# A slot plan for batches 3 to 8 of a fused window attention and SMELU network

## The chip, the cores and the metric

The kernel runs on one core of one Trainium2 chip. The metric is device microseconds (us) per execution, over the whole program: loads, attention, both matrix products, stores. Two sources of time are used: the median of three timed runs, and one profiled execution, from which every duration of a single instruction comes.

## The reference

```python
def _attn_ref(q, k, v):                       # 8 batches, 8 heads, 576 positions, head size 64
    scores = np.matmul(q, k.transpose(0, 1, 3, 2)) / np.sqrt(64)
    pos = np.arange(576)
    mask = np.abs(pos[:, None] - pos[None, :]) <= 32
    scores = np.where(mask, scores, -1000000000.0)
    attn = np.exp(scores - np.max(scores, axis=-1, keepdims=True))
    attn = attn / (np.sum(attn, axis=-1, keepdims=True) + 1e-09)
    return np.matmul(attn, v)
...
def _moe_ref(x, w_in, w_out):                 # x: 4608 tokens of 512; w_in 512 x 2048; w_out 2048 x 512
    h = x @ w_in
    g = np.where(h >= 1, h, np.where(h <= -1, 0.0, (h + 1) ** 2 / 4.0))
    return g @ w_out
```

The attention of each head looks only at positions at most 32 away. Its output, heads side by side, is the token matrix x (576 tokens per batch), and the SMELU network follows. All inputs and the output are float32 in memory; the kernel multiplies in bf16 and sums in float32.

## The kernel before

**Engines and the work.** TensorE does every product. ScalarE (ACT) does exponentials, logarithms, copies out of PSUM and half of SMELU. VectorE (DVE) does masks, normalisation and the other half. GpSimd (POOL) issues loads; SyncE (SP) issues stores and DMA transposes.

**The slot.** The outer loop (line 505) runs over 160 slots. Slots 0 to 143 each project a piece of tokens with `w_in`: up to slot 55 and from slot 136 a slot takes 256 tokens and 256 of the 2048 hidden columns (eight 128x256 matmuls, line 499); slots 56 to 135, the wide ones, take 512 tokens and 128 hidden columns (four 128x512 matmuls, line 524). Each fills one PSUM tile `hp`; the pool `ps_h` has two of them, so the projection of slot a needs the tile of slot a-2 to be free. SMELU of a slot has two forms. In a **plain** slot ScalarE makes `rr` = relu(h/2 + 1/2) (line 543), VectorE makes `mx` = max(h, rr) (line 549) and `gT` = min(rr, 1) * mx (line 550): `hp` is free after `mx`. In a **ScalarE-heavier** slot, named by the set `two_on_act`, ScalarE also squares `rr` (line 546) and VectorE does one operation (line 547): `hp` is free only after that.

**The products with w_out.** A unit (lines 441 to 464) is one 128x512 matmul of `gT` with `w_out`; sixteen make one tile of 128 tokens in a PSUM tile of `ps_o` (two buffers), which ScalarE copies out (line 463) and SyncE stores. Units are numbered through all tiles, and each slot issues the next few: four in slots 24 to 39, three in slots 40 to 71, four from slot 72 (lines 559 to 563; `post` before slot 40). The first 64 units' worth of work is done as "pairs" up to slot 23.

**The attention.** Each batch after the first is cut into five steps (`steps`, line 399). A step has a `scores` part and a `sums` part. `scores` (line 215): TensorE products of q and k, ScalarE `exp` into `pt` (line 239; line 268 for the tail of the sequence), VectorE mask (line 205) and, but for the tail, an addition `both` (line 244). `sums` (line 273): TensorE products of `pt` with v and with ones, then ScalarE `Ln` and `Exp` of minus that (lines 310 and 311: one over the sum), and a VectorE multiplication into the token matrix `xT` (lines 316 and 319). That multiplication is put off: `flush` issues it at the beginning of the next slot, ahead of that slot's `mx`. The list `sl` (line 420) holds one slot per remaining step; at slot `sl[n]`, between the projection and the units, `run` (line 483) issues the sums of step n and the scores of step n+1, which I call a **session**. A projection reads `xT` of all its tokens, so a session must be far enough ahead of the slot that needs it. Scores take one two-bank PSUM tile (`ps_s`) and sums another (`ps_n`).

**Loads.** For batches 3 to 7 `loads` names the slots at which GpSimd issues q, k and v, and `xps` those at which SyncE issues the DMA transposes of q and k. Neither queue waits for a slot as such: an instruction waits only for its place in the queue, its buffer and its data. Batches are numbered from 0 in the code, so "batches 3 to 8" of the change are b = 2 to 7.

**What sets the order.** The schedule is written by hand (`manual_schedule`): each engine runs its instructions in the order in which the program issues them, and the numbers in `sl`, `two_on_act`, the units per slot, `loads` and `xps` are the plan.

Of the kernel before, what the change touches and what calls it, by code (L numbers as in the profile page):

```python
# [14 lines left out]
def kernel(  # L15
# [20 lines left out]
    B, H, S, D = q.shape  # L36
    NT, DM, DFF = out.shape[0], 512, 2048
# [3 lines left out]
    MAIN = 480  # L41
    TAIL = S - MAIN
# [7 lines left out]
    nat = ctx.enter_context(tc.tile_pool(name="nat", bufs=2))  # L50
# [6 lines left out]
    ps_s = ctx.enter_context(tc.tile_pool(name="ps_s", bufs=1, space=bass.MemoryType.PSUM))  # L57
    ps_n = ctx.enter_context(tc.tile_pool(name="ps_n", bufs=1, space=bass.MemoryType.PSUM))
# [6 lines left out]
    band = const.tile([128, 192], BF, name="band")  # L65
# [7 lines left out]
    qTs = [const.tile([128, PAD + NY * S], BF, name=f"qT{i}") for i in range(3)]  # L73

    ctx.enter_context(tc.manual_schedule())
    V, P, A = nc.vector, nc.gpsimd, nc.scalar


# [24 lines left out]
    def load_v(b, n):  # L103
        if b not in vn:
            vn[b] = nat.tile([128, 2 * NC, 2, D], BF, name="vn", tag="vn", bufs=3)
        h, a = divmod(n, 2)
        y = NY * h + 2 * a
        nc.gpsimd.dma_start(out=vn[b][64 * a:64 * a + 64, :, h], in_=v[b, y:y + 2].rearrange("y s d -> (y s) d")  # L108
                            .rearrange("(c r) d -> r c d", r=64))
# [15 lines left out]
    for h in range(2):  # L125
# [8 lines left out]
    load_v(0, 0)  # L134
    P.affine_select(out=step, in_=step, compare_op=ALU.is_ge, fill=-1.0, base=-65, channel_multiplier=-1,
                    pattern=[[1, 257]])
    for n in range(1, 4):
        load_v(0, n)
    V.memset(ones, 1.0)
    for t in qTs:  # L140
        V.memset(t[:, 0:PAD], 0.0)
# [1 line left out]
    V.tensor_sub(band, step[:, 65:], step[:, :192])  # L143
    V.tensor_scalar(bias, band, 1.0, 2.0 ** 100, op0=ALU.subtract, op1=ALU.mult)

    def put(todo):
        for fn, *x in todo:
            fn(*x)

    cuts = [0, 256, 512, 768, 1024, 1280, 1536, DFF]  # L150
    w = [(load_w_in, c0, c1, h) for c0, c1 in zip(cuts, cuts[1:]) for h in range(2)]
    w[3] += ((0, 52, 64),)
    put(w[:4] + [(load_half, 1, t, h) for t in range(2) for h in range(2)] + w[4:])
    put([(load_w_out, 0, k, k + 4) for k in (0, 4, 8)] + [(load_rows, 1, t) for t in range(2)] + [(load_w_out, 0, 12, 16)])
    put([(load_v, 1, n) for n in range(4)])
    P.tensor_copy(band[HD[1], 0:128], band[HD[1], 64:192])
    for m, n, x in ((mask4, 8, 128), (mask8, 4, TAIL)):
        P.tensor_copy(m.rearrange("p (n j) -> p n j", n=n),
                      band[:, :x].rearrange("p (n j) -> p n j", n=1).to_broadcast([128, n, x]))
    put([(load_w_out, 1, 8 * n, 8 * n + 8) for n in range(2)])  # L160
    put([(load_nat, 2, t) for t in range(2)] + [(load_v, 2, n) for n in range(4)])


    kT = {}

# [221 lines left out]

    NB = NT // TB
    NF = DFF // 256
    pairs = [(7, 0), (7, 1), (8, 2), (11, 4), (12, 5), (13, 3), (15, 6), (15, 8), (16, 7), (17, 9)]  # L390
    two_on_act = (1, 7, 10, 11, 12)
    ev = {}

    def at(a, *todo):


        ev.setdefault(a, []).extend(x for x in todo if x)
# [5 lines left out]
                yield (sums, b, y1, lo, hi), (scores, b, (y1, y1 + 1), (0, 2), (2 * k, 2 * k + 2))  # L403
        yield (sums, b, 0, MAIN, S), (scores8, b)

    at(1, (tposes, 0, (0, 1), (1, 1)))
    at(2, (scores, 0, (0, 1), (0, 2), (2, 4)), (scores8, 0, ps_o))
    at(3, (scores, 0, (1, 2), (0, 2), (2, 4), ps_n), (sums, 0, 0, TB, MAIN, ps_s))
    at(4, (sums, 0, 1, TB, MAIN))
    at(5, (sums, 0, 0, MAIN, S, ps_s))  # L410
    seq = [x for b in range(1, B) for x in steps(b, CUT)]
    at(12.5, seq[0][1])
    at(13, (*seq[1][1], ps_n))
    at(14, (*seq[0][0], ps_s), seq[1][0])
    at(16, seq[2][1])
    for n, a in enumerate((18, 20, 26.5, 28)):
        at(a, seq[2 + n][0])
    for n, a in enumerate((18, 20, 26.5, 28)):
        at(a, seq[3 + n][1])
    sl = [30, 32, 35, 39, 42, 45, 47, 50, 52, 57, 60, 63, 66, 68, 72, 76, 79, 82, 86]  # L420
    sl += [90, 93, 96, 100, 104, 108, 111, 114, 118, 123]
    for n, a in enumerate(sl):
        at(a, seq[6 + n][0], seq[7 + n][1] if n < len(sl) - 1 else None)
    for t in range(2):
        at(10 + 1.5 * t, (tposes, 1, (t, 0), (t, 1)))
    two_on_act += tuple(a + 2 for a in sl)
    loads, xps = {}, {16: [(2, 0)], 18: [(2, 1)]}
    for b in range(LONG + 1, B):
        a = sl[5 * (b - 1) - 7] - 17
        for t in range(3):  # L430
            loads.setdefault(a + t, []).append((b, t))
        for t in range(2):
            xps.setdefault(a + 6 + 2 * t, []).append((b, t))

    op = {}

# [4 lines left out]
    def unit(x):  # L441

        tt, j = divmod(x, 16)
        if tt == NT // 128 - 1:
            half, n = divmod(j, 8)
            if n == 0:
                op[tt] = ps_o.tile([128, 256], FP, name="op", tag="op")
            cols = slice(256 * half, 256 * half + 256)
            for k in (2 * n, 2 * n + 1):
                nc.tensor.matmul(op[tt], gT[:, k, home(tt // 2), 128 * (tt % 2):128 * (tt % 2) + 128], w_out[:, k, cols],  # L450
                                 start=k == 0, stop=k == 15)
            if n == 7:
                osb = osp.tile([128, 256], FP, name="osb")
                A.copy(osb, op[tt])
                nc.sync.dma_start(out=out[128 * tt:128 * tt + 128, cols], in_=osb)
            return
        if j == 0:
            op[tt] = ps_o.tile([128, DM], FP, name="op", tag="op")
        nc.tensor.matmul(op[tt], gT[:, j, home(tt // 2), 128 * (tt % 2):128 * (tt % 2) + 128], w_out[:, j],  # L459
                         start=j == 0, stop=j == 15)  # L460
        if j == 15:
            osb = osp.tile([128, DM], FP, name="osb")
            A.copy(osb, op[tt])  # L463
            nc.sync.dma_start(out=out[128 * tt:128 * tt + 128, :], in_=osb)
# [18 lines left out]
    def run(pos):  # L483
        todo = []
        for fn, *x in ev.get(pos, []):
            if fn is sums:
                todo.append(sums(*x))
            elif fn is tposes:
                tposes(*x)
            else:  # L490
                pool = (x.pop(),) if x[-1] in (ps_s, ps_n, ps_o) else ()
                fn(*x, eng, *pool)
        for end in todo:
            end()

# [5 lines left out]
                             skip_group_check=True)  # L501

    hps = []
    done = 4 * (40 - NF)
    for a in range(NF * NB + 2 * NF):
        wide = WIDE[0] <= a < WIDE[1]
        eng = None if a < 14 else V
        post = [] if a >= 40 else [x for n, x in pairs if n == a] + [a - NF] * (a >= 2 * NF + 2)
        for b, x in loads.get(a, []):
            if x < 2:  # L510
                load_nat(b, x)
# [38 lines left out]
                V.scalar_tensor_tensor(g, rr, 1.0, mx, op0=ALU.min, op1=ALU.mult)  # L550
        flush()
        run(a)
        for x in post:
            if x < 16:
                pair(x)
            else:
                for j in range(4):
                    unit(4 * x + j)
        if a >= 40:
            n = 3 if a < 72 else 4  # L560
            for x in range(done, done + n):
                unit(x)
            done += n
        run(a + 0.5)
        for x in xps.get(a, []):
            xpose(*x)
# [30 lines left out]
```

## Time and profile before

| What | Value |
|---|---|
| median of three runs | 307.9 us (307.62 to 308.05) |
| profiled execution, whole time | 307.01 us |
| span of its profile (first to last instruction) | 305.2 us |
| granted TensorE clock | 1.00 throughout |
| VectorE busy | 232.4 us, 144 SMELU slots among it: 110 plain, 34 ScalarE-heavier |
| ScalarE busy | 208.0 us |
| TensorE, first matmul to last start | 1.19 to 301.55 us |
| slot 29 starts (its projection) | 72.86 us |
| slot 56, the first wide one, starts | 124.24 us |
| slot 144 onwards: only units | from about 287 us |

The profile gives each instruction's busy time, the idle time before it, and what released it. A matmul's listed duration (0.38 us for 128x512) is its latency: matmuls are pipelined, and the distance from one start to the next (0.216 us for the same one) is what it costs the engine. So the share "PE 97%" does not tell whether TensorE loses time; the starts do.

### The profile page before, as it was taken

The numbers are of one execution on the slowest core, as the hardware profiler recorded it, in microseconds if no ns is written. First come the engines' busy times: TensorE is split into PE (matmuls) and PEld (weight loads), VectorE is DVE, ScalarE is ACT, GpSimd is POOL, SyncE is SP. The second block draws the span as 40 slices with busy tenths as digits, with TensorE's granted clock in tenths as the row PEclk, the third lists the DMA queues.
The fourth block names the chain that finished last, engine by engine and source line by source line (L and its number), as shares of the span: only waits on it lengthen the run. The fifth ranks groups of instructions, "written<-read, shape, count | busy, mean of one in ns | idle before, by whom it ended". The sixth has DMA issues, their size and how long they took to land.

```text
span 305.2 us, 7779 instructions
## 1 busy us (share of the span) xinstructions
PE 296.6 (97%) x3268; PEld 172.1 (56%) x3268; DVE 232.4 (76%) x377; ACT 208.0 (68%) x347; POOL 77.5 (25%) x93
## 2 busy tenths in 40 slices
PE   8889999999999999999999999999999999999995
PEld 3467878876566667545444444444445444446644
DVE  4269878989888898999888878877888877788700
ACT  3677786738877888788877877786778755444311
POOL 8895771019008107303700640000000000000000
PEclk9999999999999999999999999999999999999999
DMA  9999999999999999996999998570101000000121
GB/s 151 182 180 200 187 183 172 173 165 147 135 213 90 172 159 128 150 147 121 165 133 156 120 173 82 113 114 34 37 34 38 37 35 37 35 34 34 63 77 69
DMA packets 137251, 35.66 MB, mean 117 GB/s; under 512 B 122240, under 2 KB 132992, under 8 KB 137216
## 3 DMA queue, kind: packets, MB, share of 16 engines
q0 software_dynamic: 103056, 18.06, 80.5%
q1 hardware_dynamic: 34016, 16.81, 27.2%
q8 instruction: 25, 0.41, 0.6%
q10 hardware_dynamic: 144, 0.29, 0.4%
q14 instruction: 10, 0.08, 0.1%
HBM read 36.70 MB, written 9.44 MB: 151 GB/s over the span
## 4 chain that ended last, share of the span: by engine, by line
PE 84%; DMA 4%; DVE 4%; POOL 4%; ACT 2%; issue 1%; POOLq 0%; ACTq 0%
PE op L459 33%; PE hp L524 23%; PE hp L499 14%; PE op L474 5%; PE bb L304 5%; DMA w_in<-in_moe_w_in_dram 4%; POOL w_in L113 2%; PE bb L231 2%; DVE mx L549 1%; PE op L450 1%; POOL vn L108 1%; ACT pt L239 1%; DVE gT L550 1%; PE tp L191 1%; DVE xT L316 1%
## 5 line engine op out<-in xcount | busy, mean ns | idle before, releaser
L543 ACT ACTIVATE rr<-hp 128x512 f32<-128x512 f32 x144 | 85.5, 594 | 68.5 <-PE hp L524 37.7
L459 PE MATMUL op<-w_out,gT 128*128 128x512 bf16 x496 | 127.0, 380 | 0.0
L549 DVE TENSOR_TENSOR mx<-hp,rr 128x512 f32<-128x512 f32 x110 | 75.8, 689 | 26.1 <-ACT rr L543 25.3
L524 PE MATMUL hp<-xT,w_in 128*128 128x512 bf16 x320 | 82.1, 379 | 0.0
L550 DVE SCALAR_TENSOR_TENSOR gT<-rr,mx 128x512 bf16<-128x512 f32 x110 | 76.4, 694 | 3.8
L459 PEld LDWEIGHTS <-gT 128*128 128x128 bf16 x496 | 46.0, 98 | 47.6
L499 PE MATMUL hp<-xT,w_in 128*128 128x256 bf16 x512 | 66.4, 273 | 3.3 <-DMA w_in<-in_moe_w_in_dram 2.1
L499 PEld LDWEIGHTS <-w_in 128*128 128x128 bf16 x512 | 49.1, 98 | 19.0 <-issue 3.2
L524 PEld LDWEIGHTS <-w_in 128*128 128x128 bf16 x320 | 31.2, 98 | 38.2 <-issue 0.9
L100 POOL DMA_DIRECT2D qn<-in_q_dram x12 | 14.6, 1223 | 91.7 <-DMA kT<-kn 89.6
L239 ACT ACTIVATE pt<-bb 128x1024 bf16<-128x1024 f32 (+1 forms) x33 | 32.8, 999 | 3.5 <-PE bb L231 2.2
L547 DVE SCALAR_TENSOR_TENSOR gT<-hp,mx 128x512 bf16<-128x512 f32 x34 | 23.5, 690 | 13.9 <-ACT mx L546 13.6
L108 POOL DMA_DIRECT2D vn<-in_v_dram x32 | 27.5, 893 | 6.1 <-DMA w_out<-in_moe_w_out_dram 3.2
L463 ACT COPY osb<-op 128x512 f32<-128x512 f32 x31 | 18.0, 579 | 12.0 <-PE op L459 11.6
L316 DVE TENSOR_TENSOR xT<-bb,rc 128x512 bf16<-128x512 f32 (+1 forms) x32 | 20.9, 654 | 5.7 <-ACT rc L311 5.6
L311 ACT ACTIVATE rc<-lr 128x512 f32<-128x512 f32 (+2 forms) x40 | 23.5, 588 | 1.3
L310 ACT ACTIVATE lr<-bb 128x512 f32<-128x512 f32 (+2 forms) x40 | 22.0, 550 | 0.2 <-PE bb L304 0.2
L546 ACT ACTIVATE mx<-rr 128x512 f32<-128x512 f32 x34 | 21.4, 630 | 1.1
L205 DVE TENSOR_TENSOR pt<-pt,mask 128x1024 bf16<-128x1024 bf16 (+1 forms) x33 | 20.3, 615 | 1.4 <-ACT pt L239 1.4
L304 PE MATMUL bb<-pt,vn 64*64 64x128 bf16 (+3 forms) x712 | 18.7, 207 | 0.0
L304 PEld LDWEIGHTS <-vn 64*64 64x64 bf16 x712 | 14.7, 107 | 4.9 <-issue 4.7
L474 PE MATMUL op<-w_out,gT 128*128 128x256 bf16 x128 | 16.4, 273 | 0.0
(63 smaller groups left out, 167.2 us busy)
## 6 DMA issues: line engine op xcount, KB each, us to landing
out_dram<-osb SPq DMA_DIRECT2D x35, 256.0 KB, 2.8
vn<-in_v_dram POOLq DMA_DIRECT2D x32, 144.0 KB, 11.2
qn<-in_q_dram POOLq DMA_DIRECT2D x12, 288.0 KB, 6.2
kn<-in_k_dram POOLq DMA_DIRECT2D x12, 288.0 KB, 8.8
w_in<-in_moe_w_in_dram POOLq DMA_DIRECT2D x11, 128.0 KB, 5.1
w_out<-in_moe_w_out_dram POOLq DMA_DIRECT2D x4, 256.0 KB, 9.2
w_out<-in_moe_w_out_dram POOLq DMA_DIRECT2D x2, 512.0 KB, 12.3
kh<-in_k_dram POOLq DMA_DIRECT2D x4, 144.0 KB, 5.1
```

Source lines behind the costliest of these rows:

```text
L108: nc.gpsimd.dma_start(out=vn[b][64 * a:64 * a + 64, :, h], in_=v[b, y:y + 2].rearrange("y s d -> (y s) d") .rearrange("(c r) d -> r c d", ...
L239: A.activation(p, ps[:, :, :w * n].rearrange(like, y=m), AF.Exp, scale=D ** -0.5)
L304: nc.tensor.matmul(bb[HD[h], a, o + c0:o + c1], ones[HD[a]] if c is None else vn[b][HD[a], c, h], p(a, h), start=n == 0, stop=True, skip_g ...
L311: A.activation(rc[:, :, :D0], lr[:, :, :D0], AF.Exp, scale=-1.0)
L316: muls.append(lambda: V.tensor_mul(o, bb[:, :, :D0], rc[:, :, :D0]))
L459: nc.tensor.matmul(op[tt], gT[:, j, home(tt // 2), 128 * (tt % 2):128 * (tt % 2) + 128], w_out[:, j], start=j == 0, stop=j == 15)
L474: nc.tensor.matmul(o[:, tt], gT[:, j, p, 128 * tt:128 * tt + 128], w_out[:, j, 256 * half:256 * half + 256], start=not done, stop=len(done ...
L499: nc.tensor.matmul(hp[:, j], w_in[:, kk, 256 * f + 128 * j:256 * f + 128 * j + 128], xT[:, kk, r0:r0 + TB], start=first and n == 0, stop=l ...
L524: nc.tensor.matmul(hp.rearrange("p n t -> p (n t)"), w_in[:, kk, 128 * f:128 * f + 128], xT[:, kk, r0:r0 + 2 * TB], start=n == 0, stop=n == 3)
L543: A.activation(rr, hp, AF.Relu, scale=0.5, bias=0.5)
L549: V.tensor_max(mx, hp, rr)
L550: V.scalar_tensor_tensor(g, rr, 1.0, mx, op0=ALU.min, op1=ALU.mult)
```

## The change

The number of instructions on TensorE, GpSimd and SyncE stays the same. From slot 24 on the plan has other numbers, now in tables:

- **Sessions.** `sl` has as many entries, 29, at other slots: the second and third move from 32 and 35 to 35 and 37, for instance, and the last from 123 to 117. In the wide slots sessions lie between 58 and 117 instead of 57 and 123.
- **ScalarE-heavier slots.** `two_on_act` was "two slots after every session" and becomes a list: 24 slots in all instead of 34. From slot 29 on there are 19 instead of 29, six of them after the last session (122, 123, 126, 127, 131, 132).
- **Units.** `units` gives 0 to 7 per slot. The running total differs from that of before by at most four, and is the same at the end.
- **Order in a session.** At the slots of `ends_first` the logarithm and its `Exp` come ahead of the exponential of the new scores. Of its eight slots only 49 and 89 hold a session.
- **Loads and transposes.** They get other slots. The order on the queues of GpSimd and SyncE, instruction by instruction, is the same as before.
- The lists `LOADS`, `early_items` and `pairs` write out what was computed; up to slot 23 nothing changes but the slot of one batch's loads.

```diff
-    two_on_act = (1, 7, 10, 11, 12)
...
-    sl = [30, 32, 35, 39, 42, 45, 47, 50, 52, 57, 60, 63, 66, 68, 72, 76, 79, 82, 86]
-    sl += [90, 93, 96, 100, 104, 108, 111, 114, 118, 123]
+    two_on_act = [1, 7, 10, 11, 12, 30, 34, 41, 44, 47, 51, 59, 62, 64, 74, 90, 96, 109, 122, 123, 126, 127, 131, 132]
+    sl = [30, 35, 37, 39, 42, 45, 47, 49, 52, 58, 60, 63, 65, 68, 71, 77, 79, 81, 85, 89, 92, 95, 101, 103, 108, 110, 112, 115, 117]
+    first_sl = 6
+    bias_until = 14
+    ends_first = [36, 49, 75, 89, 93, 116, 118, 123]
     for n, a in enumerate(sl):
-        at(a, seq[6 + n][0], seq[7 + n][1] if n < len(sl) - 1 else None)
...
+        at(a, seq[first_sl + n][0], seq[first_sl + 1 + n][1] if first_sl + 1 + n < len(seq) else None)
-    two_on_act += tuple(a + 2 for a in sl)
...
-        a = sl[5 * (b - 1) - 7] - 17
+        a = [20, 31, 49, 72, 88][b - 3]
...
-            xps.setdefault(a + 6 + 2 * t, []).append((b, t))
+            xps.setdefault([[28, 30], [40, 44], [58, 59], [75, 79], [91, 98]][b - 3][t], []).append((b, t))
...
             if fn is sums:
                 todo.append(sums(*x))
+                if pos in ends_first:
+                    todo.pop()()
...
-    done = 4 * (40 - NF)
+    done = 64
+    units = [0, 0, 0, 0, 0, 0, 0, 0, 0, 0, 0, 0, 0, 0, 0, 0, 0, 0, 0, 0, 0, 0, 0, 0, 5, 3, 5, 4, 5, 3, 6, 5, 0, 4, 4, 5, 4, 4, 3, 3, 3, 4, 3, 3, 3, 3, 2, 4, 3, 1, 5, 3, 2, 3, 4, 3, 2, 3, 4, 2, 4, 3, 3, 3, 4, 3, 3, 2, 4, 3, 4, 1, 4, 6, 2, 5, 2, 4, 5, 3, 4, 4, 5, 4, 6, 2, 2, 7, 2, 4, 6, 4, 4, 2, 4, 3, 5, 4, 5, 4, 6, 1, 3, 6, 4, 5, 4, 3, 3, 5, 5, 2, 4, 7, 2, 4, 0, 4, 5, 6, 3, 6, 3, 7, 4, 2, 5, 4, 3, 4, 4, 4, 4, 4, 5, 4, 2, 4, 6, 3, 4, 3, 4, 4, 5, 2, 4, 4, 6, 5, 4, 5, 3, 2, 3, 3, 4, 7, 4, 4]
...
-        if a >= 40:
-            n = 3 if a < 72 else 4
-            for x in range(done, done + n):
-                unit(x)
-            done += n
+        for x in range(done, done + units[a]):
+            unit(x)
+        done += units[a]
```

## Prediction

> **What bounds the kernel now.** I read the page first. TensorE is busy 97% and carries 84% of the chain that ended last; VectorE and ScalarE are busy 76% and 68%.
>
> ```profile
> PE 296.6 (97%) x3268; PEld 172.1 (56%) x3268; DVE 232.4 (76%) x377; ACT 208.0 (68%) x347; POOL 77.5 (25%) x93
> ...
> PE 84%; DMA 4%; DVE 4%; POOL 4%; ACT 2%; issue 1%; POOLq 0%; ACTq 0%
> ```
>
> The busy share counts latency, so I went to the timeline of TensorE and looked at starts. Four w_out products take 0.864 us from first start to next work, eight narrow projection matmuls 0.87, four wide ones 0.864: 0.216 us per 512 columns, with nothing between. So TensorE streams, and the question is only where it does not. From slot 29 on I find seven places where a projection starts later than the work before it allows. The largest is slot 32, the second slot 50:
>
> ```profile
> 77.95 1.03 PE L459 MATMUL op<-w_out,gT 128*128 128x512 bf16 x4
> 78.82 0.38 PE L499 MATMUL hp<-xT,w_in 128*128 128x256 bf16 x2
> 79.76 0.81 PE L499 MATMUL hp<-xT,w_in 128*128 128x256 bf16 x6 [0.56 <-DVE xT L316]
> ```
>
> ```profile
> 110.98 0.81 PE L459 MATMUL op<-w_out,gT 128*128 128x512 bf16 x3
> 111.63 1.04 PE L499 MATMUL hp<-xT,w_in 128*128 128x256 bf16 x8
> 112.50 0.81 PE L459 MATMUL op<-w_out,gT 128*128 128x512 bf16 x3
> 113.55 1.03 PE L499 MATMUL hp<-xT,w_in 128*128 128x256 bf16 x8 [0.24 <-DVE mx L549]
> ```
>
> In slot 32 two matmuls start from 78.82, so the third was due at 79.04; it starts at 79.76 when VectorE has written `xT`: 0.72 us lost. In slot 50 three units from 112.50 take 0.65 us (110.98 to 111.63 shows it), so 113.15 was due and 113.55 came: 0.40. The same reading gives 0.17 at 122.72 (slot 55), 0.07 at 131.11 and 136.46 (60, 63), 0.09 at 141.87 (66) and 0.19 at 151.01 (71). All others lose at most 0.03. The sum, 1.71 us, is all that a new order of the same matmuls can win: number and shape of TensorE's 3268 matmuls stay, and what is lost before slot 29 (the w_in loads at 14.8, 18.4 and 26.1) is untouched.
>
> **What the change costs, engine by engine.** Ten slots become plain. Each gives VectorE one more operation (`mx`, 0.69 us) and takes a square (0.63) from ScalarE: VectorE +6.9 us busy, ScalarE -6.3. Whether that costs anything depends on how closely VectorE can run, which the burst after a session shows:
>
> ```profile
> 236.37 0.69 DVE L550 SCALAR_TENSOR_TENSOR gT<-rr,mx 128x512 bf16<-128x512 f32 x1
> 236.98 0.69 DVE L205 TENSOR_TENSOR pt<-pt,mask 128x1024 bf16<-128x1024 bf16 x1
> 237.70 0.42 DVE L244 TENSOR_TENSOR both<-pt 128x512 bf16<-128x512 bf16 x1
> 238.04 0.69 DVE L316 TENSOR_TENSOR xT<-bb,rc 128x512 bf16<-128x512 f32 x1
> 238.65 0.68 DVE L549 TENSOR_TENSOR mx<-hp,rr 128x512 f32<-128x512 f32 x1
> 239.36 0.69 DVE L550 SCALAR_TENSOR_TENSOR gT<-rr,mx 128x512 bf16<-128x512 f32 x1
> ```
>
> The reader is to see the starts: an operation that needs its predecessor follows after 0.72 us, an independent one already after 0.61 (0.34 after `both`), 0.08 before the listed end. So a plain slot costs VectorE 0.72 + 0.61 = 1.33 us, a ScalarE-heavier one 0.61, a session 0.72 + 0.34 + 0.60 = 1.66 (tail scores: 0.28 for mask and no `both`). TensorE's side: 0.87 per projection, 0.216 per unit, about 0.75 for a session (slot 73 before: 2.48 us from projection to projection, its neighbours 1.73).
>
> I summed both over stretches of the new plan. Slots 64 to 71: TensorE 8 x 0.87 + 24 x 0.216 + 2.2 for three sessions = 14.3 us; VectorE 7 x 1.33 + 0.61 + 2.3 (masks, `both`) + 1.7 (`xT`) = 13.9 (before: 13.5 and 11.4). Slots 81 to 89: 17.8 against 15.3. Slots 108 to 117, five sessions: 19.9 against 18.2. ScalarE stays below 15 in all of these. Nowhere does VectorE need more than TensorE gives; over the worst short stretch (66 to 72) it falls back 0.8 us. Between sessions the projection comes 1.07 us after its tile is free (`mx` of slot 126 ends 259.03, the projection of slot 128 starts 260.10), so 0.8 is covered. **Throughput: nothing; what it costs if that cover fails is the second rival.**
>
> **Latency around sessions** is what makes the small losses. From the last score matmul run, `exp`, `Ln`, `Exp`, `xT` and the next slot's `mx` follow each other: after the session of slot 42 scores end at 100.29, `mx` at 103.92, so 3.63. The projection three slots on comes after two projections and the units of three slots: 1.74 + 0.216 U. With U = 9 that is 3.68: 0.05 to spare. Before, all ten sessions of the three-unit zone have U = 9; a heavier slot at the wrong place, or a copy of a finished tile (0.57), tips them over. The new plan gives U: 13, 10, 10 (slots 35, 37, 39), 9, 9, 8, 9, 9 (42 to 52), 10, 10, 10, 8, 11, 11 (58 to 71), and 10 or more later, but for 8 at 115. The two eights at 65 and 115 are tail sessions, whose `exp` takes 0.49 instead of 1.02 us; the eight at 47 has the next session within its three slots.
>
> - Slot 32: the session of slot 30 stays, but 11 units instead of 8 lie between its scores and slot 32: +0.65 us, and one more unit has been done by slot 29 (0.22, which delays both). Square first: `rr` about 75.9 to 76.5, square to 77.1, `exp` from 77.05, `Ln`, `Exp` to 79.1, mask from 78.1 and `both`, `xT` 79.1 to 79.75. The third matmul of slot 32 is due at 79.9. 0.72 goes. What is late next: slot 33 follows with no unit between, at 80.55, and its tile is free at about 80.4; slot 34 has 0.2 to spare.
> - Slot 50: ScalarE runs without pause from 105.72 (session 45) to `rr` of slot 48 at 112.08. From that session to slot 50 TensorE now has 13 units instead of 15 but one session more: -0.43 + 0.65 = +0.22. 0.18 of the 0.40 stays.
> - Slot 52: from session 49 (tail; `Ln` first) I get `mx` of slot 50 at 117.1 against a projection due at 117.0: 0.1.
> - Slots 55, 60, 63, 66, 71: the square leaves slot 52 (now 51, so the session's `exp` starts 0.4 earlier), and U is 9 there but 10 to 11 at 58, 60, 63, 68: 0.216 more each, against 0.07 to 0.19. All go: 0.59.
> - Heavier slots hold their tile longer: `rr` + square + 0.69 + gaps = 2.18 against 0.87 + 0.216 (two slots' units). That needs 6.1 units or a session between; 4 to 5 plus session at 30 to 64, 7 at 74, 10 and 11 at 122 and 123 hold it. 96 has 0.1 to spare.
>
> Remaining: 0.28 worked out, and I add 0.2 for what such sums miss in slots with 0.1 to 0.2 to spare. Bounds: 0 (all the new spaces hold) to 1.7 (every one that has at most 0.2 to spare fails by as much as slot 71 did, 0.19, nine times). Sum: 1.71 - 0.48 = **1.2 us won**.
>
> **Moved loads and transposes**: nothing. All five batches' loads wait for the transpose before them, not for a place in the program (GpSimd waits 89.6 us for `kT<-kn`, five times), and both queues keep their order. Transposed k lands at 115.95 for batch 4, its scores start at 118.53; after the change about 0.85 earlier, 117.7, still 1.7 us behind. For batch 7 the k transpose now waits for a store one slot later (before: 200.70, landed 206.35); scores at about 212.3. The end (units, copy, store from 287) is the same.
>
> **A rule against it.** VectorE waits 25.3 us for `rr` at line 549 and 13.6 us for squares at line 547, so it has room for 6.9. The Trainium skill (Perfetto Trace Analysis, section Identifying the Most-Contended Engine) says that matmul occupancy does not measure TensorE's distance from its limit, and that occupancy does for VectorE. By that, VectorE with its 76% would be the engine to relieve, and this change loads it: the rule's sum would be up to +6.9 us. The starts 0.216 us apart speak for TensorE, and I go by them.
>
> **Rivals.**
> 1. The gain is eaten by new small waits. Twenty-five sessions with a tenth or two to spare each; for it speaks that U varies by slot and sessions now follow at two slots' distance; against it that spaces are wider than before nearly everywhere. If 1.1 to 1.7 remains instead of 0.48, it gives 307.3 to 307.9, say 307.5.
> 2. VectorE becomes the bound, slower. If independent operations in dense stretches followed after their listed time plus 0.035 us (plain slot 1.45, session 1.9 to 2.0), slots 36 to 72 would need 4.1 us more VectorE than TensorE time (before: 1.3 at most, slots 42 to 64, where 0.99 was lost). Lost there about 3.8, against 1.71 won: +2.1, 310.0. It decides from a pitch of about 0.67 on: each 0.01 more adds 0.1 to 0.15 over slots 66 to 72, whose 0.8 then passes the 1.07 and 0.3 of the sums' own error. Against it: every burst in the timeline has independent starts 0.61 apart.
> 3. It does not do what it says: "ScalarE-heavier" stands for ten such slots fewer. That is in the sums already and gives no time of its own.
>
> **Numbers.** The profiled execution took 307.01 (span 305.2 and 1.8 around it), 0.9 below the median 307.9; I apply the difference to the median: 307.9 - 1.2 = **306.7 us**, in a profile a span of about 304.0. Chances: forecast 0.66, rival 1 0.21, rival 2 0.13. 0.2% is 0.6 us, about what can be told from no change, so faster means below 307.3: 0.66; same 0.21; slower 0.13. Range: 305.9 (all 1.71 and 0.3 of scatter, as the three runs show) to 308.2 (rival 1 whole, and the scatter).
>
> **What would show it.** In the new timeline no wait for `xT` at slot 32 and at most a tenth or two at 50 and 52; projections and units back to back from slot 53 on; VectorE busy about 239, ScalarE 202; slot 144 starting some 1.2 us earlier. Wrong if the wait list shows TensorE behind line 549's successor by more than 1 us in all, above all at slots 64 to 72, 85 to 88 or 112 to 118, or behind `kT` at 52.

## The result and the profile after

The changed kernel took 305.52 us (median of 20 runs), the kernel before 307.94 beside it (20 runs). The ratio is 0.9945 with a 95% interval of 0.9926 to 0.9963: 1.7 us faster, between 1.1 and 2.3 (the two medians lie 2.4 apart and the two means 2.1, so the medians overstate it). Set against the 307.9 of the prediction, the ratio gives 306.2. Single runs spread from 304.7 to 307.5, more than the effect, so most of what follows is read from traces: there every lost tenth has a place. The profiled execution took 305.21 us, with a span of 303.4 (before 305.2).

The page of the changed kernel: busy times, the shares of the chain that ended last, and two groups of SMELU instructions on VectorE (count, then busy us and mean ns, then idle time before and its releaser). Line numbers are new: L446 is a unit, L488 and L512 the narrow and the wide projection, L295 the sums' products, L222 the scores' products, L307 the writing of `xT`, L537 and L538 the plain slot's `mx` and `gT`, L535 the one operation of a ScalarE-heavier slot.

```profile
PE 295.3 (97%) x3268; PEld 172.3 (57%) x3268; DVE 236.5 (78%) x387; ACT 200.6 (66%) x337; POOL 77.8 (26%) x93
...
PE 89%; DMA 4%; POOL 4%; DVE 1%; issue 1%; ACT 0%; POOLq 0%; ACTq 0%
...
L537 DVE TENSOR_TENSOR mx<-hp,rr 128x512 f32<-128x512 f32 x120 | 82.5, 688 | 22.6 <-ACT rr L531 21.3
...
L535 DVE SCALAR_TENSOR_TENSOR gT<-hp,mx 128x512 bf16<-128x512 f32 x24 | 16.6, 690 | 10.6 <-ACT mx L534 10.0
```

TensorE now carries 89% of the chain instead of 84%, and VectorE 1% instead of 4%: the hand-overs to VectorE that ended the idle time of TensorE have gone, although VectorE itself has become busier (236.5 us, 232.4 before).

TensorE's waits for VectorE from its first projection or score on, in the changed kernel (what it waited for: us in total, times, longest; waits for loads, all ahead of slot 29, are left out here):

```profile
PE hp L488 <- DVE xT L307: 0.5, 1, 0.5
PE bb L222 <- DVE kT L185: 0.2, 1, 0.2
PE bb L295 <- DVE xT L307: 0.2, 1, 0.2
```

The first two lie ahead of slot 29, at 13.4 and 8.5 us, in the part that the change does not touch. From slot 29 on one wait is left, in the sums of the session at slot 47. Slot 32, the largest loss before, shows how one went; TensorE's timeline (start, us, line, tiles, count):

```profile
77.39 1.04 PE L488 MATMUL hp<-xT,w_in 128*128 128x256 bf16 x8
78.26 1.24 PE L446 MATMUL op<-w_out,gT 128*128 128x512 bf16 x5
79.34 1.91 PE L488 MATMUL hp<-xT,w_in 128*128 128x256 bf16 x16
```

Five units take 5 x 0.216 = 1.08, and 78.26 + 1.08 = 79.34: slot 32 starts when it can, and its sixteen matmuls (slot 32 gives no units, so slot 33 joins it) run as one group. `xT` was written from 78.81 to 79.43, in time for the third of them. The wait that is left, in TensorE's timeline and in VectorE's:

```profile
106.08 0.59 PE L446 MATMUL op<-w_out,gT 128*128 128x512 bf16 x2
106.51 1.04 PE L488 MATMUL hp<-xT,w_in 128*128 128x256 bf16 x8
107.70 0.31 PE L295 MATMUL bb<-pt,vn 64*64 64x128 bf16 x8 [0.15 <-DVE xT L307]
```

```profile
104.63 0.69 DVE L537 TENSOR_TENSOR mx<-hp,rr 128x512 f32<-128x512 f32 x1 [0.17 <-ACT rr L531]
105.36 0.69 DVE L538 SCALAR_TENSOR_TENSOR gT<-rr,mx 128x512 bf16<-128x512 f32 x1
105.97 0.68 DVE L196 TENSOR_TENSOR pt<-pt,mask 128x1024 bf16<-128x1024 bf16 x1
106.68 0.42 DVE L235 TENSOR_TENSOR both<-pt 128x512 bf16<-128x512 bf16 x1
107.03 0.62 DVE L307 TENSOR_TENSOR xT<-bb,rc 128x448 bf16<-128x448 f32 x1
```

The sums of session 47 were due 0.96 after the projection (0.87, and 0.09 to the sums as elsewhere), at 107.47; they came at 107.70: 0.22 lost (the bracket says 0.15, since it counts from the modelled end of the matmuls). What they wait for is not `xT` as data. The sums have one PSUM tile (`ps_n`), and it is free only when session 45's `xT` has been read out of it, at 107.65. Slots 45 and 46 give 3 + 2 units where they gave 3 + 3, and one unit, 0.216, is the whole wait.

Where the time went, by starts on TensorE:

| Start of | before | after | difference |
|---|---|---|---|
| slot 24 | 62.60 | 62.26 | -0.34 |
| slot 29 | 72.86 | 72.95 | +0.09 (two more units are done by then: +0.43) |
| slot 40 | 95.63 | 94.35 | -1.28 |
| slot 56 | 124.24 | 122.83 | -1.41 |
| slot 104 | 214.43 | 213.38 | -1.05 |
| slot 143 | 286.07 | 284.06 | -2.01 |
| last matmul | 301.55 | 299.75 | -1.80 |
| slot 29 to last | 228.70 | 226.81 | -1.89 |

Between slots the running number of units differs by up to four, 0.86 us, so single rows swing; the last row is the clean one. Of its 1.89, 0.43 are the two units that moved ahead of slot 29. The rest, 1.46, is close to what the waits say: 1.71 before, 0.22 after. Of the 1.80 between the two profiled executions, 0.34 lie ahead of slot 24, where both kernels do the same work.

That gives a measure for every kernel below. Without waits the stretch from slot 29 to the last matmul would be 228.70 - 1.71 = 226.99 us with the even units of before, and 226.81 - 0.22 = 226.59 with the new ones. What a kernel's stretch has above that is **lost by the stretch**; what single starts show, as in the prediction, is **lost by starts**. Both come from the starts of one trace and the measure is set by the two complete traces, so they check each other place by place and are not independent proofs.

### The profile page after: what moved, and what is told of

Its sections match the earlier page's. It is cut to its first block, busy times and chain, and to the rows that moved or that the text cites. A ratio compares the mean times of both kernels' runs of the same rounds, so it can differ in the third digit from the quotient of the medians.

```text
span 303.4 us, 7774 instructions
## 1 busy us (share of the span) xinstructions
PE 295.3 (97%) x3268; PEld 172.3 (57%) x3268; DVE 236.5 (78%) x387; ACT 200.6 (66%) x337; POOL 77.8 (26%) x93
## 4 chain that ended last, share of the span: by engine, by line
PE 89%; DMA 4%; POOL 4%; DVE 1%; issue 1%; ACT 0%; POOLq 0%; ACTq 0%
PE op L446 36%; PE hp L512 23%; PE hp L488 16%; PE bb L295 5%; PE op L461 5%; DMA w_in<-in_moe_w_in_dram 4%; PE bb L222 2%; POOL w_in L114 2%; POOL vn L109 1%; PE op L437 1%; PE tp L182 1%; POOL kh L88 0%; DVE mx L537 0%; DVE gT L538 0%; PE bb L201 0%
## 5 line engine op out<-in xcount | busy, mean ns | idle before, releaser
L446 PE MATMUL op<-w_out,gT 128*128 128x512 bf16 x496 | 126.6, 380 | 0.0
L537 DVE TENSOR_TENSOR mx<-hp,rr 128x512 f32<-128x512 f32 x120 | 82.5, 688 | 22.6 <-ACT rr L531 21.3
L538 DVE SCALAR_TENSOR_TENSOR gT<-rr,mx 128x512 bf16<-128x512 f32 x120 | 83.3, 694 | 4.1
L512 PE MATMUL hp<-xT,w_in 128*128 128x512 bf16 x320 | 82.0, 379 | 0.0
L446 PEld LDWEIGHTS <-gT 128*128 128x128 bf16 x496 | 46.2, 98 | 48.2
L488 PE MATMUL hp<-xT,w_in 128*128 128x256 bf16 x512 | 66.1, 273 | 1.9 <-DMA w_in<-in_moe_w_in_dram 1.5
L488 PEld LDWEIGHTS <-w_in 128*128 128x128 bf16 x512 | 49.2, 98 | 17.0 <-DMA w_in<-in_moe_w_in_dram 1.6
L512 PEld LDWEIGHTS <-w_in 128*128 128x128 bf16 x320 | 31.3, 98 | 37.6
L307 DVE TENSOR_TENSOR xT<-bb,rc 128x512 bf16<-128x512 f32 (+1 forms) x32 | 20.9, 652 | 5.7 <-ACT rc L302 5.7
L535 DVE SCALAR_TENSOR_TENSOR gT<-hp,mx 128x512 bf16<-128x512 f32 x24 | 16.6, 690 | 10.6 <-ACT mx L534 10.0
L302 ACT ACTIVATE rc<-lr 128x512 f32<-128x512 f32 (+2 forms) x40 | 23.5, 587 | 1.3
L295 PE MATMUL bb<-pt,vn 64*64 64x128 bf16 (+3 forms) x712 | 18.7, 206 | 0.3 <-DVE xT L307 0.2
L295 PEld LDWEIGHTS <-vn 64*64 64x64 bf16 x712 | 14.8, 107 | 5.1 <-issue 4.7
L534 ACT ACTIVATE mx<-rr 128x512 f32<-128x512 f32 x24 | 15.1, 630 | 0.8
```

Source lines behind the costliest of these rows:

```text
L295: nc.tensor.matmul(bb[HD[h], a, o + c0:o + c1], ones[HD[a]] if c is None else vn[b][HD[a], c, h], p(a, h), start=n == 0, stop=True, skip_g ...
L302: A.activation(rc[:, :, :D0], lr[:, :, :D0], AF.Exp, scale=-1.0)
L488: nc.tensor.matmul(hp[:, j], w_in[:, kk, 256 * f + 128 * j:256 * f + 128 * j + 128], xT[:, kk, r0:r0 + TB], start=first and n == 0, stop=l ...
L512: nc.tensor.matmul(hp.rearrange("p n t -> p (n t)"), w_in[:, kk, 128 * f:128 * f + 128], xT[:, kk, r0:r0 + 2 * TB], start=n == 0, stop=n == 3)
L537: V.tensor_max(mx, hp, rr)
```

## The experiments

Theory 1 (T1) is the prediction's: TensorE streams, each loss is a session's chain of ScalarE and VectorE coming too late for one start, and the plan widens the spaces; so parts of it, alone, should leave or make losses at nameable places. Rivals: the gain comes from one part alone; or fewer VectorE operations decide; or lost time is only moved. Diffs are against the changed kernel. "Old" means the numbers of before.

| Kernel | sessions | ScalarE-heavier | units | lost by starts | lost by the stretch | time, us (beside it: before) |
|---|---|---|---|---|---|---|
| before | old | old | old | 1.71 | | 307.94 (20 runs) |
| e1 | new | old rule | old | 1.92 | 1.94 | 307.25 (307.66) |
| e5 | old | new | old | 2.10 | 2.11 | 306.97 (306.71) |
| e6 | old | old | new | 2.76 | 2.71 | 309.18 (306.71) |
| e2 | new | new | old | 1.55 | 1.57 | 307.66 (307.66) |
| e3 | new | old rule | new | 1.66 | 1.63 | 306.03 (307.66) |
| e7 | old | new | new | 2.37 | 2.33 | 311.02 (306.71) |
| after | new | new | new | 0.22 | | 305.52 (307.94, 20 runs) |

e5, e6 and e7 also have the old slots for loads and transposes and no `ends_first`; e11 tests those parts. The times of e1 to e3 and e5 to e7 are single runs, and their differences lie largely ahead of slot 29: in e7 slot 24 starts at 65.96 instead of 62.26. It waits longer for `w_in` (first line of TensorE's waits that concerns a load; 1.5 us in all in the changed kernel):

```profile
PE hp L488 <- DMA w_in<-in_moe_w_in_dram: 3.8, 3, 2.0
```

The wait of 2.0 ends with slot 6's projection at 27.88 us, 2.1 later than in the changed kernel, and behind it the granted clock over 28 to 32 us is 0.57 (1.00 in the changed kernel): slot 6 to slot 8 takes 5.17 us instead of 3.59. So 3.7 of e7's 311.02 comes from the load phase, ahead of all that the plan changes; the two "lost" columns are what counts in this table.

### e1: the new sessions alone

```diff
-    two_on_act = [1, 7, 10, 11, 12, 30, 34, 41, ...]
+    two_on_act = [1, 7, 10, 11, 12, 32, 37, 39, 41, ...]
-    units = [0, ..., 5, 3, 5, 4, 5, 3, 6, 5, 0, ...]
+    units = [0] * 24 + [4] * 16 + [3] * 32 + [4] * 88
```

> New session slots only; units as before (4 in slots 24 to 39, 3 in 40 to 71, 4 after) and ScalarE-heavier slots two behind each session as before. Measure: time that TensorE loses from slot 29 on, summed over starts of a projection or of a session that come later than the work before them allows (before: 1.71 us, changed kernel: 0.22). Theory 1 (the three parts win only together: a session needs about nine units up to the projection three slots on, and a heavier slot must not stand in or behind it): 1.3 to 2.3 us lost, slot 32's 0.72 still among it. Rival A (moving the sessions carries the gain): below 0.6.

Lost 1.92: 0.72 at slot 32, 0.40 at 42, 0.36 in the sums of session 49, 0.07 at 56, 0.31 at 62, 0.05 in the sums of session 65. As T1 had it; the rival, that sessions alone are the gain, falls. The loss at slot 50 has become one at 49, by the same PSUM tile as above (TensorE's timeline of e1):

```profile
112.02 1.04 PE L488 MATMUL hp<-xT,w_in 128*128 128x256 bf16 x8
113.35 0.31 PE L295 MATMUL bb<-pt,vn 64*64 64x128 bf16 x8 [0.29 <-DVE xT L307]
```

### e2: everything but the units

```diff
-    units = [0, ..., 5, 3, 5, 4, 5, 3, 6, 5, 0, ...]
+    units = [0] * 24 + [4] * 16 + [3] * 32 + [4] * 88
```

> The changed kernel with even units (4, 3, 4 per slot as before). Theory 1: slot 32's wait of about 0.7 is back (8 units instead of 11 between session 30 and slot 32), and small ones of 0.05 to 0.1 in slots 40 to 71 where nine units stand behind a session: 0.7 to 1.4 us lost in all from slot 29 on. Rival A (sessions and heavier slots carry the gain, uneven units are ornament): below 0.4. Session 47 has three units instead of two two slots before it, so its wait of 0.22 goes by either.

Lost 1.55: 0.57 at 32, 0.36 in session 49, 0.16 at 62, 0.37 at 97, and small ones. A little above the expected 1.4. Slot 97 was not foreseen; TensorE's timeline there:

```profile
202.83 1.03 PE L446 MATMUL op<-w_out,gT 128*128 128x512 bf16 x4
204.06 1.02 PE L512 MATMUL hp<-xT,w_in 128*128 128x512 bf16 x4 [0.21 <-DVE gT L535]
```

The releaser L535 is the VectorE operation of a ScalarE-heavier slot. With even units its tile is free 0.37 too late for the next but one projection. The prediction had given slot 96 "0.1 to spare" with the new units. The heavier slots are placed for these units, and cost something without them.

### e3: the ScalarE-heavier slots two behind each session

```diff
-    two_on_act = [1, 7, 10, 11, 12, 30, 34, 41, ...]
+    two_on_act = [1, 7, 10, 11, 12, 32, 37, 39, 41, ...]
```

> The changed kernel, but ScalarE-heavier slots are two behind each session, by the rule of before (29 from slot 29 on instead of 19, VectorE about 7 us less busy, ScalarE 6 more). Theory 1: 0.5 to 1.6 us lost from slot 29 on, since seven heavier slots then fall into a session's own slot and hold its exponential back by a square. Rival B (VectorE's load is what matters, the fewer plain slots the better): 0.2 or less. Rival C (occupancy: relieving the busiest engine beside TensorE, VectorE, wins): below 0.2 and the span shorter than that of the changed kernel.

Lost 1.66: 0.50 at slot 34, 0.29 at 52, 0.25 at 67, 0.23 in session 47, 0.17 in session 81 and small ones. Just above T1's 1.6; what the rivals had does not occur. (Twelve heavier slots fall into a session's own slot, not the seven that I had counted.) The ten slots are thus no free choice: 29 heavier slots at the wrong places lose 1.4 us more than 19 at the right ones.

### e4: no ScalarE-heavier slot from slot 29 on

```diff
-    two_on_act = [1, 7, 10, 11, 12, 30, 34, 41, ...]
+    two_on_act = [1, 7, 10, 11, 12]
```

> The changed kernel with no ScalarE-heavier slot from slot 29 on: 19 more VectorE operations (13 us more busy), ScalarE 12 less. Theory 1 (independent VectorE operations follow 0.61 apart): over slots 38 to 72 VectorE needs 2.0 us more than TensorE gives, about 1.07 is covered: 0.8 to 1.8 us lost from slot 29 on, 0.2 to 0.6% slower than the changed kernel. Rival D (listed durations plus the gap count, VectorE is near its bound): 6 us or more lost.

This is the test of VectorE as the bound. First line of the page of e4:

```profile
PE 291.5 (96%) x3227; PEld 172.9 (57%) x3268; DVE 247.5 (81%) x406; ACT 189.6 (62%) x318; POOL 77.7 (26%) x93
```

VectorE is busy 11.0 us longer than in the changed kernel (247.5 against 236.5). Lost is 1.22 by starts, 1.29 by the stretch, 1.0 to 1.1 more than in the changed kernel and as T1 had it. By time, 306.74 (10 runs) against 307.66: ratio 0.999, 0.9952 to 1.0027. So eleven more microseconds of VectorE cost one. Nor is that one a matter of throughput: it lies at six places, the largest the sums of session 47, 0.42, where slot 44 and its successors are now plain (due 105.96 + 0.96 = 106.92):

```profile
105.96 1.04 PE L488 MATMUL hp<-xT,w_in 128*128 128x256 bf16 x8
107.34 0.31 PE L295 MATMUL bb<-pt,vn 64*64 64x128 bf16 x8 [0.35 <-DVE xT L307]
```

(41 matmul records are missing here, 3227 of 3268, and 38 or 41 in the trace of every other experiment; gaps of one matmul, 0.215 to 0.23, without a releaser are those and are not counted.) The rival of 6 us and more falls: in this kernel VectorE's 76 to 81% is not nearness to a limit.

### e5: the new ScalarE-heavier slots alone

Old `sl`, old slots of loads and transposes, old units and no `ends_first` (the line of the transposes is left out below):

```diff
-    sl = [30, 35, 37, 39, 42, 45, 47, 49, 52, ...]
+    sl = [30, 32, 35, 39, 42, 45, 47, 50, 52, ...]
-    ends_first = [36, 49, 75, 89, 93, 116, 118, 123]
+    ends_first = []
-        a = [20, 31, 49, 72, 88][b - 3]
+        a = [22, 35, 51, 69, 87][b - 3]
...
-    units = [0, ..., 5, 3, 5, 4, 5, 3, 6, 5, 0, ...]
+    units = [0] * 24 + [4] * 16 + [3] * 32 + [4] * 88
```

> Sessions and units as before, only the new list of ScalarE-heavier slots (ten fewer). Measure: time that TensorE loses from slot 29 on (before 1.71, changed kernel 0.22). Theory 1 (the parts win only together): slot 32's 0.72 and slot 50's 0.40 stay, those of 55 and 71 go, slot 64 now stands right behind session 63 and costs 0.2 to 0.4 at 66: 1.3 to 2.0 us lost. Rival B (the new list carries the gain, since a heavier slot holds its tile longer): below 0.6.

Lost 2.10: 0.57 at 32, 0.40 at 50, 0.28 at the scores of slot 52 (waiting for the DMA transpose of k), 0.06 and 0.07 at 60 and 63, 0.54 at 66, 0.18 at 71. That is just above T1's 2.0; without the wait for the transpose, which is not the heavier slots' doing as far as is known (see e11), it is 1.82. In detail T1 was wrong twice: 66 costs more than the 0.2 to 0.4 that I had, and the loss at 71 did not go. Slot 64 is now ScalarE-heavier, two ahead of it, with no session between:

```profile
140.66 0.81 PE L446 MATMUL op<-w_out,gT 128*128 128x512 bf16 x3
141.84 1.02 PE L512 MATMUL hp<-xT,w_in 128*128 128x512 bf16 x4 [0.37 <-DVE gT L535]
```

### e6: the new units alone

As e5, but with the new `units` and old heavier slots.

> Sessions and ScalarE-heavier slots as before, only the new units per slot. Theory 1: the units are cut to the new sessions; with the old ones slot 32 is cured, but 35 (eight units behind session 32, with a heavier slot between) and 50 (13 units instead of 15 since session 45 and no session between) lose more: 1.5 to 3.0 us lost from slot 29 on, slower than before. Rival A (uneven units as such fill the holes): below 0.8.

Lost 2.76, the most of all. The largest is 0.74 at slot 117 (TensorE's timeline of e6; the wait is put down to `mx`):

```profile
239.64 1.03 PE L512 MATMUL hp<-xT,w_in 128*128 128x512 bf16 x4
241.25 1.02 PE L512 MATMUL hp<-xT,w_in 128*128 128x512 bf16 x4 [0.58 <-DVE mx L537]
```

Two projections follow each other: slot 116 gives no unit. The new sessions lie at 112, 115 and 117; the old plan has one at 114, and slots 114 to 116 give 2 + 4 + 0 = 6 units. By the prediction's formula that is 1.74 + 0.216 x 6 = 3.04 us against 3.63, 0.59 too early; 0.74 was lost. I had not foreseen the place, though the formula has it. Of the places that I named, 35 lost 0.63, and 50 with 0.42 hardly more than before. The uneven units are no gain of their own.

### e7: the old sessions, with the new units and heavier slots

As e5, but with the new `units`.

> The changed kernel with the session slots of before (new units and new list of heavier slots). Theory 1: 1.5 to 2.6 us lost from slot 29 on. Rival A (units and heavier slots carry the gain, where sessions stand matters little): below 0.6.

Lost 2.37 by starts, 2.33 by the stretch: 0.75 at 117 again, 0.42 at 50, 0.32 at 66, 0.29 at 35, 0.22 each in session 47 and at 72, 0.08 and 0.07 at 60 and 96. As T1 had it.

**What e1 to e7 say together.** One part alone loses 1.9, 2.1 and 2.8; two of three lose 1.6, 1.7 and 2.3 to 2.4; before lost 1.71 and all three lose 0.22. No part gives a gain that the others add to: each is fitted to the others, and the gain is there when all three are.

### e8 and e9: can the last 0.22 go?

e8 gives the missing unit back to slot 46 from 47; e9 takes it from slot 50.

```diff
 # e8: units[46], units[47]
-    2, 4
+    3, 3
 # e9: units[46], units[50]
-    2, 5
+    3, 4
```

> The changed kernel with one unit moved from slot 47 to slot 46 (3 and 3 instead of 2 and 4). Theory 1: session 47 waits 0.22 us in the changed kernel because the sums' PSUM tile of session 45 is free only when xT is written; one more unit (0.216) ahead of it covers that, nothing behind it moves (the running total after slot 47 is the same), but the projection of slot 50 then has only 0.07 to spare: 0 to 0.1 us lost from slot 29 on, the stretch from there 0.1 to 0.2 us shorter than in the changed kernel; by time 0.05% and not to be told from it. Rival E (the wait is ScalarE's, which runs without pause from session 45 to slot 48, and only moves): 0.2 lost at slot 50 instead.

> The changed kernel with one unit moved from slot 50 to slot 46. Taking it from slot 47 moved the 0.22 us wait of session 47 to session 49 (0.36). Theory 2 (from session 45 to slot 50 TensorE runs against a chain of ScalarE and VectorE work that does not move; only work of TensorE brought in ahead of session 47 from behind slot 50 helps): no wait at 47, 49 or 50, at most 0.05 at the projection of slot 52, stretch from slot 29 to the last matmul 0.15 to 0.25 us shorter than in the changed kernel; in the time 0.07%, not to be told from it. Rival (ScalarE's chain is fixed to TensorE's own starts): 0.1 to 0.4 lost at 49 or 52 again.

e8 lost 0.36, now in the sums of session 49; nothing at 47. T1's 0 to 0.1 is wrong, the rival's "it moves" is right, though not in its place. Due at 110.52 + 0.96 = 111.48, come at 111.86:

```profile
110.52 1.04 PE L488 MATMUL hp<-xT,w_in 128*128 128x256 bf16 x8
111.86 0.31 PE L295 MATMUL bb<-pt,vn 64*64 64x128 bf16 x8 [0.29 <-DVE xT L307]
```

e9 leaves three units each in slots 47 and 48 and takes the unit from behind the sessions. It lost 0.15 in session 49 and 0.08 at slot 52, 0.23 in all; my second theory, that 0 to 0.05 is left, falls as well, and its rival holds: from session 45 to slot 52 ScalarE and VectorE set the pace, and in the three plans tried 0.22 to 0.36 stays. In e9's timeline session 49's sums were due at 111.54 + 0.96 = 112.50, and slot 52 at 116.04 + 0.65 = 116.69:

```profile
111.54 1.04 PE L488 MATMUL hp<-xT,w_in 128*128 128x256 bf16 x8
112.65 0.31 PE L295 MATMUL bb<-pt,vn 64*64 64x128 bf16 x8
...
116.04 0.81 PE L446 MATMUL op<-w_out,gT 128*128 128x512 bf16 x3
116.77 1.03 PE L488 MATMUL hp<-xT,w_in 128*128 128x256 bf16 x8
```

There is no bracket, since the losses are shorter than the modelled latency of the matmuls ahead; only starts show them. Times: e8 305.90 (12 runs; ratio to before 0.9973, 0.995 to 0.9996), e9 305.81 (12 runs; 0.9958, 0.9935 to 0.9981). Neither differs measurably from the changed kernel.

### e10: a tile of its own for q and for k

On top of e9. The two tiles into which GpSimd loads q and k are exchanged with each batch, so that q of a batch goes where k of the batch before was, and waits for that k's transpose. With tiles of their own q follows q and k follows k:

```diff
-        x = dst[b] = nat.tile(..., tag=f"n{(b + t) % 2}", bufs=1)
+        x = dst[b] = nat.tile(..., tag=f"n{t}", bufs=1)
```

> As the run with one unit moved from slot 50 to 46, and the raw q and raw k of batches 2 to 7 have an SBUF tile each instead of swapping two: the load of q then waits for the transpose of the q before it, not for that of k, which lands 1.6 to 3.4 us later. Theory 3 (the chain load, transpose, load reaches slot 52 with 0 to 3 us to spare, depending on the execution: k of batch 4 landed at 114.4 to 118.2 us in the profiles so far, its scores start at 117.3 to 118.5): transposed k of batch 4 lands at 113 or earlier, those behind it earlier too, no wait for it at slot 52; time 0 to 0.2% shorter than the run without this edit. Rival: the loads are bound by the DMA engines themselves (busy 90% up to 200 us), k lands when it did, time the same.

Transposed k of batch 4 landed at 113.0 (e9: 115.4, the changed kernel: 114.39), its scores started at 116.67: 3.7 us of cover. That of batch 5 landed at 132.8 instead of e9's 139.1, so the rival's "k lands when it did" fails, while its "time the same" holds. The losses stayed 0.23 at the same places, time 305.21 (12 runs; ratio 0.9959, 0.9935 to 0.9984), which can't be told from e9's. Earlier transposes bring no measurable time where they are hidden.

### e11: the small parts of the change undone

Old slots for loads and transposes, no `ends_first`, the six heavier slots after the last session plain (the line of the transposes is left out below).

```diff
-    two_on_act = [..., 90, 96, 109, 122, 123, 126, 127, 131, 132]
+    two_on_act = [..., 90, 96, 109]
-    ends_first = [36, 49, 75, 89, 93, 116, 118, 123]
+    ends_first = []
-        a = [20, 31, 49, 72, 88][b - 3]
+        a = [22, 35, 51, 69, 87][b - 3]
```

> The changed kernel without its small parts, which act at different places: loads and transposes at the slots of the old rule, no logarithm ahead of the exponential at 49 and 89, the six ScalarE-heavier slots behind the last session plain. Theory 1: nothing of it counts: 0.22 us lost from slot 29 on as in the changed kernel, at session 47; at 52 or 91 up to 0.2 more without the early logarithm. Rival (the loads' new slots matter): a wait for transposed k at 52, 85 or 103 of 0.3 us or more.

At slots 49, 89 and from 122 on nothing is lost: in this trace `ends_first` and the six late heavier slots do nothing for the time. 0.22 in session 47 stays. But 1.23 appears in the session of slot 52, at the first scores of batch 4 (TensorE's timeline of e11):

```profile
117.62 0.20 PE L295 MATMUL bb<-pt,vn 64*64 64x64 bf16 x4
118.88 0.42 PE L222 MATMUL bb<-qT,kT 64*64 64x128 bf16 x16 [1.05 <-DMA kT<-kn]
```

The scores start 0.03 after the last group of the sums where nothing is missing (117.25 and 117.28 in the changed kernel), so they were due at 117.65; the bracket's 1.05 counts from the modelled end of the matmuls. With the 0.22 that makes 1.45 lost by starts, 1.46 by the stretch; time 306.82, one run, beside 306.54 for the kernel before. By the number the rival holds, with a cause of its own: k landed at 118.8. Is that the moved loads? Over the profiled executions k of batch 4 landed at 115.9 to 119.7 with the old load slots (before, e5, e6, e7, e11) and at 114.0 to 117.4 with the new (after, e1 to e4, e8, e9, e12). The two sets overlap. For this batch the orders on the two queues are the same in both, so I know no way by which the slots could act. Most of e11's lateness was there a batch earlier: transposed k of batch 3 landed at 93.2 instead of 90.0, and GpSimd issues the next q only after it (at 93.77 and 90.59). Whether e11's 1.23 is the slots or the scatter of these transfers stays open; one trace of each kernel does not tell.

### e12: eight units behind the session of slot 92

A direct test of the prediction's formula: two units move from slots 92 and 94 to 90 and 91, so that U is 8 instead of 10 behind a full session in the wide slots, where the formula gives a loss and the plan has none.

```diff
 # units[90] to units[94]
-    6, 4, 4, 2, 4
+    7, 5, 3, 2, 3
```

> The changed kernel with two units taken from slots 92 and 94 to slots 90 and 91: the session of slot 92 then has 8 units up to the projection of slot 95 instead of 10. Theory 1 (projection three slots on comes 1.74 + 0.216 U after the scores, the chain behind them takes 3.63; in the changed kernel the tile was free 0.20 us ahead): 0.15 to 0.25 us lost at slot 95, nothing elsewhere beside the 0.22 at session 47. Rival (slack in the wide slots is larger than that, VectorE catches up): 0 to 0.05.

One new loss, where it was to be, 0.29 at slot 95, a little above T1's 0.25 (due 194.85 + 0.65 = 195.50; TensorE's timeline, then the `mx` of slot 93 in VectorE's):

```profile
193.99 1.03 PE L512 MATMUL hp<-xT,w_in 128*128 128x512 bf16 x4
194.85 0.81 PE L446 MATMUL op<-w_out,gT 128*128 128x512 bf16 x3
195.79 1.02 PE L512 MATMUL hp<-xT,w_in 128*128 128x512 bf16 x4
```

```profile
195.05 0.68 DVE L537 TENSOR_TENSOR mx<-hp,rr 128x512 f32<-128x512 f32 x1
```

Slot 95 had 0.20 to spare in the changed kernel, and two units are 0.43: 0.23 was to be lost, 0.29 was. The 0.06 between is the hand-over: `mx` ends at 195.73, and the projection starts at 195.79. 0.22 at session 47 is there too, 0.50 by the stretch. Time 305.56, one run.

## Why the prediction was right, and where it was off

- **What bounds.** Right. TensorE's stream of 0.216 us per 512 columns is the limit and what an order can win is what the starts lose. All seven places named are free of loss in the changed kernel: 32, 50, 55, 60, 63, 66, 71.
- **The size.** 1.2 us was forecast, 1.46 came by the stretch and 1.7 (1.1 to 2.3) by the ratio. The term that was mis-sized is "Remaining: 0.48": it measured 0.22. The 0.18 at slot 50 and 0.1 at slot 52 did not occur, and the 0.2 for what the sums miss was not needed. The 0.22 lies at a place that the prediction does not name, so that it comes near the 0.28 worked out is luck. I had counted when `hp` tiles come free, and not when the one tile of the sums does, which sessions two slots apart (45 and 47) make the closer of the two. The loss at 47 delays what follows by 0.22, and slot 50 has 0.30 to spare (slot 48's `mx` ends at 112.23, the projection starts at 112.53). In e8, where session 47 does not wait, slot 50 would have been due at 112.27 but for the new wait at 49, with its tile free only at 112.40: the loss that I forecast there lies hidden behind another. So e8 and e9 agree: the loss goes from place to place and hardly shrinks.
- **The formula 1.74 + 0.216 U against 3.63.** Right in form, and its 3.63 is 0.13 to 0.15 too short in the wide slots. By itself it gives 0.16 lost in e12 and 0.59 in e6; 0.29 and 0.74 were measured. There the chain from the end of the scores to the end of `mx` takes 3.69 and 3.73, and the projection starts 0.05 to 0.06 after that, a hand-over that the formula leaves out.
- **Throughput: nothing.** Right, and the clearest result. VectorE's pitches are unchanged (104.63, 105.36, 105.97 above: 0.73 to a dependent operation, 0.61 to an independent one, against 0.72 and 0.61), and e4 puts 11 us more on VectorE for a loss of 1.0 to 1.1. So the second rival falls, and so does the price of up to 6.9 us under "A rule against it". That price used one half of what the Trainium skill says (Perfetto Trace Analysis, section Identifying the Most-Contended Engine). For TensorE the section puts two measures in place of matmul occupancy, the matmul work done against the peak and the busy share of the weight loads, and the prediction uses neither. An estimate from the starts stands in for the first: the matmuls with `w_in` and `w_out` alone, 816 of 512 columns at 0.216 us and 672 of 256 at 0.109, fill about 250 of the 305.2 us before, 82%, more than VectorE's 76%. The section, read whole, is thus not refuted by this case; no run here tests it further.
- **VectorE busy "about 239".** It is 236.5. The SMELU operations' own times rose from 75.8 + 76.4 + 23.5 to 82.5 + 83.3 + 16.6 us, by 6.7, near the 6.9 worked out; but busy time counts overlapping operations once. On VectorE an operation starts before the listed end of the one ahead 139 times instead of 113, and these overlaps sum to 11.2 us instead of 8.9; all operations' own times rose by 6.4, and 6.4 less 2.3 is the 4.1 by which the busy time grew. ScalarE: 200.6 for 202.
- **Moved loads and transposes: nothing.** Right in the changed kernel's trace: k of batch 4 landed at 114.39, the scores started at 117.28, 2.9 us later (1.7 was forecast). As a general statement it was too sure. In one trace of each kernel the cover runs from 3.7 us (e10) to 0.04 (e4), and in e5 (0.28) and e11 (1.23) it failed.
- **Rival 1**, new small waits, was right in kind and small: one instead of many. e1, e2 and e3 show that it had a basis, since the same sessions with other units or heavier slots lose 1.55 to 1.92.
- **The range.** By the ratio the time is 306.2, within 305.9 to 308.2; the ratio's interval, 305.6 to 306.8, reaches a little below it, and so does the plain median of 305.52. The 0.3 for the scatter was too small: three runs spread from 307.62 to 308.05, twenty of the same kernel from 306.02 to 309.11.

## What to carry to other kernels

Where one engine streams, read its starts: their sum against an ideal pitch is all that reordering can win, and it names the places. Then check, for each point at which the stream takes something back from another engine, every buffer that it needs, single PSUM tiles first, and not only the one that waited before. A plan of several coupled lists can be worth its gain only whole: here no list gave any by itself, and a part tested alone would have been thrown away. And a part that changes nothing visible may stand in for cover that scatters, so read more than one trace before calling a transfer hidden.

## What the runs showed of the hardware

- An independent VectorE operation starts 0.08 us before the listed end of the one ahead (0.61 against 0.69), so ten more operations of 0.69, and 26 more places where one follows another closely, raised the busy time by 4.1 us and not by 6.9. Added work is not read off the difference of two busy times.
- The load phase scatters far more than the effect studied: slot 24 starts at 61.6 to 66.0 us over the profiled executions, by waits for `w_in` (1.5 us in the changed kernel, 3.8 in e7) and `w_out` (0.98 in e9, 1.05 in e6), and in e7 by the clock: behind a wait of 2.05 us the granted clock over 28 to 32 us was 0.57, and sixteen matmuls of 256 columns took 3.04 us instead of 1.92. Much of the 304.7 to 307.5 of single runs may come from there; that was not tested by itself.
- The DMA transpose of k of batch 4 lands at 114.0 to 119.7 us over thirteen kernels, one trace of each. The load phase is part of that: from slot 24's start it is 52.1 to 56.2 us. A load waits for the transpose before it, so lateness is handed on: of the 4.4 us by which e11 is behind the changed kernel, 3.2 were there at batch 3.
